# Local attention on TensorE: values and softmax sums as one burst per block pair, with long sums between value rounds 3 and 4 and in PSUM banks of their own

## The chip, the cores and the metric

The kernel runs on one core of a Trainium2 chip. The metric is the device time of one execution in microseconds (us). Every profiled run was classed as fast, with a granted TensorE clock of 0.998 or more, so all runs can be compared. TensorE appears in the profile as PE (matmuls) and PEld (weight loads), VectorE as DVE, ScalarE as ACT.

## The reference, cut to what matters

The output is `g * a + (1 - g) * b` with x of 2048 tokens by 1024 features, 32 heads of 32. `a` is a linear-attention block, `b` a local attention. Only `b` is touched:

```python
# b: local, dilated attention: each position sees 8 positions, 2 apart
logits = einsum("bhsd,bhswd->bhsw", q, kg) * scale          # W = 8, dil = 2
logits = where(mask, logits, -1e9)
attn = softmax(logits, axis=-1)
o = einsum("bhsw,bhswd->bhsd", attn, vg)
return o.transpose(...).reshape(B, S, D) @ wo
```

The kernel splits the tokens into even and odd ones, so that a window is 8 neighbours, and works in pairs of blocks of 57 queries against 64 keys. There are 18 such pairs.

## The kernel before

All matmuls are recorded as operations with a cost in a small planner, which orders them by list scheduling. Attention bursts are strewn between the groups of 8 projection matmuls (128x512), which are the bulk of the work. A pair has a burst of logits (S, 64 matmuls) and, three planner slots later, a burst of values and sums (PV). A third kind of small burst (kv, 32 matmuls) belongs to the linear attention.

In PV the array is used in tiles of 64 rows by 32 columns (how the array is split is called its mode; the projections use it whole): `h` (which block of the pair) picks the rows, `j` the columns, so 8 tiles work side by side. A head's values take 57 columns on one tile. The sums are matmuls with a stationary block of ones.

```python
SO = banks[4:8]                       # four PSUM banks, used by S and then by PV
...                                   # S: logits, Exp on ACT, mask on DVE -> E
def values():
    for g in range(2):                # two halves of the heads
        def each(e, g=g):
            for c in range(4):
                for j in range(4):
                    for h in range(2):
                        hd = 16 * g + 4 * c + j
                        e.matmul(SO[2*g + h].ap(c*nq, (c+1)*nq)[32*j:32*j+32, :],
                                 vt[64*h:64*h+64, hd*32:hd*32+32],
                                 E[64*h:64*h+64, (8*j+4*g+c)*nq:(8*j+4*g+c+1)*nq],
                                 start=True, stop=True, tile_position=(64*h, 32*j))
            for j in range(4):
                for h in range(2):    # sums of 4 heads: 228 columns, same bank as the values
                    last = e.matmul(SO[2*g + h].ap(4*nq, 8*nq)[32*j:32*j+32, :],
                                    ones[64*h:64*h+64, :],
                                    E[64*h:64*h+64, (8*j+4*g)*nq:(8*j+4*g+4)*nq], ...)
            return last               # the semaphore is incremented with this one
        P.op("pe", each, 0.36, mode="c", ...)
        P.op("act", ... Ln of the sums ...)      # both banks of the half
        P.op("act", ... Exp(-Ln) ...)
        P.op("dve", ... values * that -> qT ...)
after(PVLAG, values)
```

(Cuts are marked with dots.)

## Time and profile before

| | before |
|---|---|
| time, median of 3 runs | 504.89 us (504.59 to 505.67) |
| profiled span | 502.5 us |
| PE busy | 488.5 us, 97% of the span |
| the chain that ended last | 95% PE |

From the page of the kernel before, part 1 (busy time by engine) and the first line of part 4 (the chain that ended last):

```profile
PE 488.5 (97%) x5190; PEld 232.6 (46%) x5257; DVE 264.6 (53%) x456; ACT 192.9 (38%) x335; POOL 6.6 (1%) x30
PE 95%; issue 2%; DMA 1%; ACT 1%; SPq 0%; DVE 0%
```

TensorE is the only engine that counts. ACT and DVE are idle half the time, and their idle time costs nothing.

The timeline of PE around the first PV burst (start in us, length in us, engine, line, operation, count):

```profile
133.06 0.81 PE L1324 MATMUL ps_all<-xT,w 128*128 128x512 bf16 x3
133.80 0.31 PE L1447 MATMUL ps_all<-E,v 64*32 64x57 bf16 x32
134.02 0.33 PE L1452 MATMUL ps_all<-E,ones 64*32 64x228 bf16 x8
134.12 0.47 PE L1447 MATMUL ps_all<-E,v 64*32 64x57 bf16 x32
134.41 0.32 PE L1452 MATMUL ps_all<-E,ones 64*32 64x228 bf16 x8
134.89 3.40 PE L1324 MATMUL ps_all<-xT,w 128*128 128x512 bf16 x15 [0.16 <-issue]
138.22 0.70 PE L1427 MATMUL ps_all<-qT,kT 32*64 32x57 bf16 x64
```

L1324 are projections, L1447 values, L1452 sums, L1427 the S burst. The 0.16 us of "issue" is no wait: 16 weight loads stand against 15 matmuls there, so the record of the first matmul is missing. Merged lines hide what matters inside a burst, so the single records are needed. These are the start times of the 80 matmuls of this burst, in ns from its first weight load, eight to a line, worked out from the trace:

```
before     0: 2 5 9 12 15 19 21 25            values g=0
           8: 40 44 48 51 54 57 61 64
          16: 69 73 77 80 83 85 90 94
          24: 99 102 106 109 111 114 119 125
          32: 225 234 243 251 259 268 275 284   sums g=0
          40: 323 340 348 356 359 364 370 373   values g=1
          48: 379 380 387 389 394 404 412 420
          56: 426 434 443 451 459 468 476 484
          64: 507 528 536 544 553 561 569 604
          72: 612 620 629 637 645 653 662 670   sums g=1
projections' first weight load: 864
```

The first 32 load/matmul pairs (64 instructions) start within 0.13 us. Then there is a hole of 0.10 us, and from there pairs come at about 8.3 ns each, with further small holes. The whole burst is 0.670 us from first to last start, then 0.194 us pass until the first projection load. I call the first number the burst and the second the exit. All 18 bursts of this kernel agree within 4 ns.

### The profile page before, as it was taken

How to read it: one execution, taken by the hardware profiler on the slowest of the kernel's cores; microseconds unless marked ns; L12 is line 12 of the kernel's file. 1: busy time of each engine (PE TensorE's matmuls, PEld its weight loads, DVE VectorE, ACT ScalarE, POOL GpSimd, SP SyncE). 2: the span in 40 equal slices, each digit the busy share in tenths (PEclk: the TensorE clock that was granted, in tenths of full speed). 3: DMA queues.
4: the chain of work that ended last, by engine and by line, in shares of the span. 5: the costliest groups of instructions: out<-in, count | busy, mean ns of one | idle time of the engine just before them, and what ended most of it. 6: DMA issues, size and time to landing. Idle time of an engine off the chain costs nothing.

```text
span 502.5 us, 11582 instructions
## 1 busy us (share of the span) xinstructions
PE 488.5 (97%) x5190; PEld 232.6 (46%) x5257; DVE 264.6 (53%) x456; ACT 192.9 (38%) x335; POOL 6.6 (1%) x30
## 2 busy tenths in 40 slices
PE   8999999999999999999999999999999999999996
PEld 2444444444454444544544545444444444444443
DVE  3112235556667676454555464678776563234443
ACT  1111111111354454655554555479864543100000
POOL 5000000000000000000000000000000000000000
PEclk9999999999999999999999999999999999999999
DMA  8999990000024060100010100500000000011222
GB/s 222 207 204 314 353 270 1 1 0 1 12 86 139 22 198 27 34 23 23 23 39 21 33 1 3 170 0 1 0 2 0 2 0 1 1 43 64 83 78 73
DMA packets 47410, 34.92 MB, mean 69 GB/s; under 512 B 22261, under 2 KB 43125, under 8 KB 47354
## 3 DMA queue, kind: packets, MB, share of 16 engines
q1 hardware_dynamic: 46810, 33.59, 23.6%
q8 instruction: 43, 0.70, 0.6%
q10 hardware_dynamic: 544, 0.52, 0.4%
q14 instruction: 13, 0.11, 0.1%
HBM read 21.51 MB, written 8.40 MB: 60 GB/s over the span
## 4 chain that ended last, share of the span: by engine, by line
PE 95%; issue 2%; DMA 1%; ACT 1%; SPq 0%; DVE 0%
PE ps_all L1324 76%; PE ps_all L1677 11%; PE ps_all L1427 2%; PE ps_all L1447 2%; PE ps_all L1602 1%; PE ps_all L1452 1%; PE ps_all L1523 1%; DMA xT<-in_A_x_dram 1%; PE ps_all L1580 1%; ACT ra L1604 0%; PE ps_all L1392 0%; SPq L1294 0%; SPq L1299 0%; ACT e L1333 0%; ACT ra L1605 0%
## 5 line engine op out<-in xcount | busy, mean ns | idle before, releaser
L1324 PE MATMUL ps_all<-w,xT 128*128 128x512 bf16 x922 | 207.8, 379 | 5.6 <-issue 4.0
L1324 PE MATMUL ps_all<-xT,w 128*128 128x512 bf16 x747 | 169.2, 379 | 2.5 <-issue 1.9
L1324 PEld LDWEIGHTS ps_all<-w,xT 128*128 128x128 bf16 x960 | 91.3, 98 | 110.3 <-issue 1.7
L1324 PEld LDWEIGHTS ps_all<-xT,w 128*128 128x128 bf16 x768 | 73.9, 98 | 88.8 <-ACT ra L1604 0.6
L1677 PE MATMUL ps_all<-w,qT 128*128 128x512 bf16 (+1 forms) x259 | 55.2, 373 | 0.3
L1677 PEld LDWEIGHTS ps_all<-w,qT 128*128 128x128 bf16 x264 | 25.8, 98 | 29.7
L1335 DVE TENSOR_SCALAR e<-e 128x512 bf16<-128x512 bf16 x64 | 18.4, 291 | 38.9 <-ACT e L1331 25.3
L1355 DVE CAST vst<-ps_all 128x512 bf16<-128x512 f32 x15 | 10.4, 691 | 42.7 <-PE ps_all L1324 42.7
L1433 ACT ACTIVATE E<-ps_all 128x1824 bf16<-128x1824 f32 (+1 forms) x18 | 30.4, 1687 | 3.1 <-PE ps_all L1427 2.0
L1331 ACT ACTIVATE e<-ps_all 128x512 bf16<-128x512 f32 x32 | 19.1, 597 | 31.6 <-PE ps_all L1324 30.8
L1333 ACT ACTIVATE e<-ps_all 128x512 bf16<-128x512 f32 x32 | 19.2, 601 | 29.3 <-PE ps_all L1324 27.8
L1681 DVE SCALAR_TENSOR_TENSOR o<-ps_all,gm,xT 128x512 bf16<-128x512 f32 (+1 forms) x25 | 18.2, 729 | 23.0 <-PE ps_all L1677 22.8
L1280 DVE TENSOR_TENSOR mx<-mx,kT 128x1024 bf16<-128x1024 bf16 x32 | 20.7, 688 | 16.9 <-ACT kT L1356 16.8
L1280 DVE TENSOR_TENSOR mx<-mx,qT 128x1024 bf16<-128x1024 bf16 x32 | 20.7, 688 | 16.7 <-ACT qT L1359 16.6
L1356 ACT ACTIVATE vst<-ps_all 128x512 bf16<-128x512 f32 x17 | 10.1, 597 | 47.8 <-PE ps_all L1324 47.8
L1436 DVE TENSOR_TENSOR E<-E,msk 128x1824 bf16<-128x1824 bf16 (+1 forms) x18 | 19.8, 1100 | 14.5 <-ACT E L1433 14.5
L1462 DVE TENSOR_TENSOR qT<-ps_all,L 128x456 bf16<-128x456 f32 (+1 forms) x36 | 21.1, 624 | 7.7 <-ACT L L1461 7.7
L1359 ACT ACTIVATE qT<-ps_all 128x512 bf16<-128x512 f32 x15 | 9.0, 597 | 37.0 <-PE ps_all L1324 37.0
L1337 DVE SCALAR_TENSOR_TENSOR pk<-ps_all,e 128x512 bf16<-128x512 f32 x32 | 22.0, 688 | 0.8
L1604 ACT ACTIVATE ra<-ps_all,eps 128x512 f32<-128x512 f32 x32 | 21.5, 688 | 2.2 <-PE ps_all L1602 2.0
L1356 ACT ACTIVATE az<-ps_all 128x512 bf16<-128x512 f32 x19 | 11.4, 600 | 27.6 <-PE ps_all L1324 27.6
L1356 ACT ACTIVATE kT<-ps_all 128x512 bf16<-128x512 f32 x14 | 8.4, 597 | 35.5 <-PE ps_all L1324 35.5
(77 smaller groups left out, 336.5 us busy)
## 6 DMA issues: line engine op xcount, KB each, us to landing
w<-in_A_wqkv_dram SPq DMA_DIRECT2D x6, 1024.0 KB, 8.2
v<-vB_hbm SPq DMA_DIRECT2D x36, 128.0 KB, 2.6
vB_hbm<-vst SPq DMA_DIRECT2D x32, 128.0 KB, 4.9
w<-in_B_wqkv_dram SPq DMA_DIRECT2D x4, 1024.0 KB, 8.3
out_dram<-o SPq DMA_DIRECT2D x15, 256.0 KB, 2.0
w<-in_A_wo_dram SPq DMA_DIRECT2D x2, 1024.0 KB, 5.6
w<-in_B_wo_dram SPq DMA_DIRECT2D x2, 1024.0 KB, 6.5
w<-in_B_wqkv_dram SPq DMA_DIRECT2D x6, 256.0 KB, 4.1
```

The source lines that it names most:

```text
L1280: P.op("dve", lambda e, m=m, op=op: e.tensor_tensor(m[:, 0:n], m[:, 0:n], src, op), 0.08 + n / 1920.0, reads=[m.all(), reg], writes=[m.all()],
L1324: last = e.matmul(bank.ap(), lhs(dc), rhs(dc), start=(dc == 0), stop=(dc == 7))
L1331: P.op("act", lambda e: e.activation(e_[:, :], bank.ap(), ACT.Exp), act(512), reads=[bank.iv], writes=[e_.all()])
L1333: P.op("act", lambda e: e.activation(e_[:, :], bank.ap(), ACT.Exp, accum_out=qe[:, col:col + 1]), act(512) + 0.1, reads=[bank.iv], writes= ...
L1335: P.op("dve", lambda e: e.tensor_scalar(e_[:, :], e_[:, :], 1.0, 1e-6, op0=ALU.min, op1=ALU.add), 0.25, reads=[e_.all()], writes=[e_.all()])
L1337: P.op("dve", lambda e: e.scalar_tensor_tensor(out=dst, in0=bank.ap(), scalar=0.0, in1=e_[:, :], op0=ALU.max, op1=ALU.add), dps(512), read ...
L1356: fa = lambda e: e.activation(dst, src(), ACT.Copy)
L1433: P.op("act", lambda e: e.activation(E[:, 0:32 * nq].rearrange("p (j q) -> p j q", j=4), ps[:, 4:8, 0:8 * nq], ACT.Exp), act(32 * nq), rea ...
L1436: P.op("dve", lambda e: e.tensor_tensor(ev(), ev(), m[:, :, :].rearrange("p r q -> p (r q)")[:, None, :].to_broadcast([128, 16, 2 * nq]), ...
L1462: P.op("dve", lambda e, L=L, pb=pb, g=g: e.tensor_tensor(qT[:, 4 * g:4 * g + 4, t0 + qs:t0 + qs + 2 * nq].rearrange("p c (h q) -> p h c q" ...
L1604: P.op("act", lambda e: e.activation(R[:, :], db.ap(), ACT.Ln, bias=eps[:, :]), act(512), reads=[db.iv, eps.all()], writes=[R.all()])
L1677: last = e.matmul(bank.ap(0, f1 - f0), qT[:, dc, t * 128:(t + 1) * 128], ws[3][:, dc, f0:f1], start=(dc == 0), stop=(dc == 7))
```

## The change

Its intent is to spend less PE time on a pair: the two halves become one burst and one operation, sums of 4 heads (228 columns, 16 matmuls) become sums of 8 heads (456 columns, 8 matmuls), and these stand between value rounds 3 and 4 (a round is 8 values, one on each tile). 456 columns of values and 456 of sums do not fit into one bank, which the kernel lays out as 512 columns, so values go to banks 0 and 1 of the four and sums to banks 2 and 3. Ln, Exp and multiply go by block `h` instead of by half of the heads, in the same number and size. The planner's cost of the burst changes from 2 x 0.36 to 0.61 us, so the order of instructions is planned anew.

```diff
-    Lr = Ring([SB([128, 2, 4 * 57], F32, "L%d" % i) for i in range(2)])
+    Lr = Ring([SB([128, 8 * 57], F32, "L%d" % i) for i in range(2)])
+    SUMS_AT = 3
 ...
-                for g in range(2):
-                    def each(e, g=g):
-                        for c in range(4): ...            # values, as shown above
-                        for j in range(4): ...            # sums, as shown above
-                        return last
-                    P.op("pe", each, 0.36, mode="c", ..., writes=bi, name="PV")
+                def each(e):
+                    def part(c):
+                        for j in range(4):
+                            for h in range(2):
+                                hd = 4 * c + j
+                                last = e.matmul(SO[h].ap(c * nq, (c + 1) * nq)[32 * j:32 * j + 32, :], vt[64 * h:64 * h + 64, hd * 32:hd * 32 + 32],
+                                                E[64 * h:64 * h + 64, (8 * j + c) * nq:(8 * j + c + 1) * nq], start=True, stop=True, tile_position=(64 * h, 32 * j))
+                        return last
+                    for c in range(SUMS_AT):
+                        part(c)
+                    for j in range(4):
+                        for h in range(2):
+                            e.matmul(SO[2 + h].ap(0, 8 * nq)[32 * j:32 * j + 32, :], ones[64 * h:64 * h + 64, :], E[64 * h:64 * h + 64, 8 * j * nq:8 * (j + 1) * nq],
+                                     start=True, stop=True, tile_position=(64 * h, 32 * j))
+                    for c in range(SUMS_AT, 8):
+                        last = part(c)
+                    return last
+                P.op("pe", each, 0.61, mode="c", ..., writes=[s.iv for s in SO], name="PV")
+                for h in range(2):
 ...                                                         # Ln, Exp, multiply by h instead of g
```

More of the change, by code (lines that the diff above doesn't have):

```diff
@@ L1439, in values @@
             def values():
-                for g in range(2):
-                    def each(e, g=g):
-                        for c in range(4):
-                            for j in range(4):
-                                for h in range(2):
-                                    hd = 16 * g + 4 * c + j
-                                    e.matmul(SO[2 * g + h].ap(c * nq, (c + 1) * nq)[32 * j:32 * j + 32, :], vt[64 * h:64 * h + 64, hd * 32:hd * 32 + 32],
-                                             E[64 * h:64 * h + 64, (8 * j + 4 * g + c) * nq:(8 * j + 4 * g + c + 1) * nq],
-                                             start=True, stop=True, tile_position=(64 * h, 32 * j))
+                def each(e):
+                    def part(c):
@@ L1450, in each @@
                         for j in range(4):
                             for h in range(2):
-                                last = e.matmul(SO[2 * g + h].ap(4 * nq, 8 * nq)[32 * j:32 * j + 32, :], ones[64 * h:64 * h + 64, :],
-                                                E[64 * h:64 * h + 64, (8 * j + 4 * g) * nq:(8 * j + 4 * g + 4) * nq],
-                                                start=True, stop=True, tile_position=(64 * h, 32 * j))
-                        return last
-                    bi = [SO[2 * g].iv, SO[2 * g + 1].iv]
@@ L1457, in values @@
-                    P.op("pe", each, 0.36, mode="c", reads=[vt.all(), ones.all(), E.all()], writes=bi, name="PV")
-                    L, _ = Lr.next()
-                    pb = lambda o, g=g: ps[:, 4 + 2 * g:6 + 2 * g, 4 * o * nq:4 * (o + 1) * nq]
-                    P.op("act", lambda e, L=L, pb=pb: e.activation(L[:, :, 0:4 * nq], pb(1), ACT.Ln), act(8 * nq), reads=bi, writes=[L.all()])
-                    P.op("act", lambda e, L=L: e.activation(L[:, :, 0:4 * nq], L[:, :, 0:4 * nq], ACT.Exp, scale=-1.0), act(8 * nq), reads=[L.all()], writes=[L.all()])
@@ L1462, in values @@
-                    P.op("dve", lambda e, L=L, pb=pb, g=g: e.tensor_tensor(
-                        qT[:, 4 * g:4 * g + 4, t0 + qs:t0 + qs + 2 * nq].rearrange("p c (h q) -> p h c q", h=2),
-                        pb(0).rearrange("p h (c q) -> p h c q", c=4), L[:, :, 0:4 * nq].rearrange("p h (c q) -> p h c q", c=4), ALU.mult), dps(8 * nq),
-                        reads=bi + [L.all()], writes=[qT.part((4 * g, 4 * g + 4), (t0 + qs, t0 + qs + 2 * nq))])
+                                hd = 4 * c + j
@@ new lines, in each @@
+                    for c in range(SUMS_AT, 8):
+                        last = part(c)
+                    return last
+                P.op("pe", each, 0.61, mode="c", reads=[vt.all(), ones.all(), E.all()], writes=[s.iv for s in SO], name="PV")
+                for h in range(2):
+                    L, _ = Lr.next()
+                    n = 8 * nq
+                    P.op("act", lambda e, L=L, h=h: e.activation(L[:, 0:n], SO[2 + h].ap(0, n), ACT.Ln), act(n), reads=[SO[2 + h].iv], writes=[L.all()])
+                    P.op("act", lambda e, L=L: e.activation(L[:, 0:n], L[:, 0:n], ACT.Exp, scale=-1.0), act(n), reads=[L.all()], writes=[L.all()])
+                    q0 = t0 + qs + h * nq
+                    P.op("dve", lambda e, L=L, h=h, q0=q0: e.tensor_tensor(
+                        qT[:, :, q0:q0 + nq], SO[h].ap(0, n).rearrange("p (c q) -> p c q", c=8), L[:, 0:n].rearrange("p (c q) -> p c q", c=8), ALU.mult), dps(n),
+                        reads=[SO[h].iv, L.all()], writes=[qT.part((0, 8), (q0, q0 + nq))])
```

## The prediction

> **What bounds the kernel.** TensorE. The page gives PE 97% of a 502.5 us span, the chain that ended last is 95% PE, the granted clock is full. The list of waits shows no PE wait on ACT or DVE in the attention stage (128 to 315 us). So a change pays only by what it takes out of the PE stream.
>
> **What one pair costs now.** In the timeline a pair's values and sums are one unbroken stretch: 32 value matmuls, 8 sums of 228 columns, 32 values, 8 sums, with 80 weight loads. From the single PE records (first pair, 133.79 us; all 18 alike):
> - entry: 0.09 us;
> - the first 32 load/matmul pairs start within 0.12 us;
> - a hole of 0.10 us before the next matmul (first sum);
> - then about 8.3 ns per pair, with a 39 ns hole where values wait for the first sums, and late holes of 23, 20 and 34 ns; last matmul at 0.67 us;
> - 0.19 us until the projections' first weight load: about 0.095 us of the last sum's columns, 0.10 us of drain.
> About 0.97 us of PE, 17.5 us for 18 pairs (3.5% of the span).
>
> The 32 fast pairs are 64 instructions. The Trainium skill, "TensorE: Matmul & The Clock Gate", table at its head, gives the engine's queue as 64 deep; the trace agrees (the hole comes after matmul 32 in PV and in S). So instruction issue bounds the burst, not columns.
>
> **What the change does.** Columns stay the same. 8 weight loads and 8 matmuls fall away: 8 x 8.3 ns = 0.066 us. Three rounds of values and the 8 long sums are exactly 64 instructions, so they issue from the full queue, and the refill hole (0.10 us) lies under the sums' stream. A sum of 228 columns held its tile 98 ns (first sum to next value), so one of 456 should hold it about 195 ns (estimate), from about 0.10 to 0.29 us. The other 40 value pairs become available at 8.3 ns each from 0.225 us, so the last starts at about 0.55 us, or 0.60 if the late holes stay. The burst now ends in a 57-column matmul, as S does, whose exit is 0.135 us, not 0.19: 0.06 us less. New cost 0.79 to 0.84 us a pair; saving 0.12 to 0.18 us, times 18: 2.2 to 3.3 us, all on the critical path.
>
> **What it could cost.** Ln starts only when the whole burst is done, so the last multiply should end 0.2 us later. Today it ends 1.17 us or more before the next S burst, so S should not wait. ACT and DVE work keeps its size (36 Ln of 0.55, 36 Exp of 0.59, 36 multiplies of 0.62 us). The order is planned anew with other costs, so a kv burst now next to PV may move (each separate one costs some 0.2 us more).
>
> **Prediction.** 502.3 us, 80% range 501.0 to 503.7. Faster by over 2%: 0.01; within 2%: 0.98; slower by over 2%: 0.01.
>
> **What the profile should show.** 72 matmuls per burst, the hole after the 32nd hidden in the sums' stream, 0.55 to 0.60 us from first to last start, first projection load 0.135 us later; S bursts unchanged at 0.50 us; no PE wait on ACT or DVE.
>
> **What would make it wrong.** Sums that block weight loads for all tiles, so that the refill does not run under them; a new order that adds mode changes or waits for banks; a late Ln chain delaying S.

## The result

The changed kernel took 501.80 us (median of 4 runs, 501.19 to 502.48) against 504.74 us for the kernel before (504.45 to 505.67, 4 runs). The ratio is 0.9942, with a 95% interval of 0.9928 to 0.9956. Here and below a ratio is the mean time of one kernel's fast runs over that of the other's of the same rounds, so it is not quite the ratio of the medians quoted. The gain is real and well inside 2%.

From the page of the changed kernel, the lines that answer to those above:

```profile
PE 493.2 (99%) x5113; PEld 231.4 (46%) x5113; DVE 267.6 (54%) x460; ACT 191.4 (38%) x331; POOL 6.6 (1%) x30
PE 96%; SPq 2%; DMA 1%; ACT 1%; issue 0%; DVE 0%
```

PE's busy time went up although the kernel got faster. That is no contradiction: the kernel before lacks about 70 matmul records, and this trace lacks none (as many matmuls as weight loads). Busy PE time is the wrong number here; the length of each stretch is the right one. The timeline of PE around the first PV burst after (L1325 projections, L1447 values, L1454 sums):

```profile
133.03 0.81 PE L1325 MATMUL ps_all<-xT,w 128*128 128x512 bf16 x3
133.76 0.28 PE L1447 MATMUL ps_all<-E,v 64*32 64x57 bf16 x24
133.86 0.38 PE L1454 MATMUL ps_all<-E,ones 64*32 64x456 bf16 x8
134.06 0.51 PE L1447 MATMUL ps_all<-E,v 64*32 64x57 bf16 x40
134.49 5.35 PE L1325 MATMUL ps_all<-xT,w 128*128 128x512 bf16 x24
```

And its single records, in ns as before:

```
after      0: 1 5 8 11 15 18 21 25            values, rounds 0 to 2
           8: 41 44 46 50 54 57 60 63
          16: 70 73 76 79 83 86 89 92
          24: 99 102 105 108 111 115 120 124    sums, 456 columns
          32: 291 294 296 300 303 306 311 316   values, rounds 3 to 7
          40: 317 321 323 326 330 334 342 351
          48: 359 367 376 384 392 401 409 417
          56: 476 484 492 501 509 517 526 534
          64: 542 551 559 567 576 584 592 601
projections' first weight load: 724
```

The burst fell from 0.670 to 0.601 us and the exit from 0.194 to 0.123 us: 0.140 us a pair.

That accounts for the whole gain. I measured from the 257th projection weight load (after the v projections) to the 1280th (after the last PV burst; one separate kv burst comes later): 256.35 us before, 253.77 us after, 2.58 us less. (The ratio above stands for 2.9 us, with 2.2 to 3.6 us for its interval; the two profiled spans differ by 2.4 us.) Sixteen pairs give 0.140 us each and the two pairs with a kv burst directly ahead give 0.104 us each, 2.45 us together. There is also one separate stretch of bursts between projections fewer (38 against 39), because one more kv burst came to stand next to a PV burst; the lengths of the stretches put that at 0.10 us. Ahead of the measured part and behind it, the two traces agree within 0.2 us.

The risk of a late Ln did not come true. From the timelines of ACT and DVE, the Ln, Exp and multiply of the first pair before and after (L1460, L1461, L1462 became L1463, L1464, L1466):

```profile
134.38 0.99 ACT L1460 ACTIVATE L<-ps_all 128x456 f32<-128x456 f32 x2 [1.61 <-PE ps_all L1452]
135.26 1.06 ACT L1461 ACTIVATE L<-L 128x456 f32<-128x456 f32 x2
135.88 1.17 DVE L1462 TENSOR_TENSOR qT<-ps_all,L 128x456 bf16<-128x456 f32 x2
```

```profile
134.64 0.99 ACT L1463 ACTIVATE L<-ps_all 128x456 f32<-128x456 f32 x2 [1.90 <-PE ps_all L1447]
135.52 1.06 ACT L1464 ACTIVATE L<-L 128x456 f32<-128x456 f32 x2
137.04 1.16 DVE L1466 TENSOR_TENSOR qT<-ps_all,L 128x456 bf16<-128x456 f32 x2
```

Ln starts 0.26 us later and the multiply over a microsecond later in this pair, yet the next S burst begins 1.58 us after the multiply's end here, and never less than 1.05 us after it in any pair. The waits of PE after the change name no engine in the attention stage:

```profile
PE ps_all L1364 <- DVE warm L1273: 1.3, 1, 1.3
PE ps_all L1325 <- DMA xT<-in_A_x_dram: 0.9, 2, 0.7
```

Both of these stand at the start of the kernel.

### The profile page after: what moved, and what is told of

Its sections match the earlier page's. It is cut to its first block, busy times and chain, and to the rows that moved or that the text cites. A ratio compares the mean times of both kernels' runs of the same rounds, so it can differ in the third digit from the quotient of the medians.

```text
span 500.1 us, 11359 instructions
## 1 busy us (share of the span) xinstructions
PE 493.2 (99%) x5113; PEld 231.4 (46%) x5113; DVE 267.6 (54%) x460; ACT 191.4 (38%) x331; POOL 6.6 (1%) x30
## 4 chain that ended last, share of the span: by engine, by line
PE 96%; SPq 2%; DMA 1%; ACT 1%; issue 0%; DVE 0%
PE ps_all L1325 76%; PE ps_all L1680 11%; PE ps_all L1428 2%; PE ps_all L1447 2%; PE ps_all L1605 1%; SPq L1295 1%; PE ps_all L1526 1%; DMA w<-in_B_wqkv_dram 1%; PE ps_all L1454 1%; PE ps_all L1583 1%; SPq L1300 1%; ACT ra L1607 0%; PE ps_all L1393 0%; ACT e L1334 0%; ACT ra L1608 0%
## 5 line engine op out<-in xcount | busy, mean ns | idle before, releaser
L1325 PE MATMUL ps_all<-w,xT 128*128 128x512 bf16 x960 | 214.2, 379 | 1.1 <-DMA xT<-in_A_x_dram 0.9
L1325 PE MATMUL ps_all<-xT,w 128*128 128x512 bf16 x768 | 172.1, 379 | 0.1
L1325 PEld LDWEIGHTS ps_all<-w,xT 128*128 128x128 bf16 x960 | 91.1, 98 | 109.9 <-DMA w<-in_B_wqkv_dram 1.4
L1325 PEld LDWEIGHTS ps_all<-xT,w 128*128 128x128 bf16 x768 | 74.1, 98 | 88.8 <-ACT ra L1607 0.6
L1466 DVE TENSOR_TENSOR qT<-ps_all,L 128x456 bf16<-128x456 f32 (+1 forms) x36 | 21.0, 627 | 6.2 <-ACT L L1464 5.0
L1463 ACT ACTIVATE L<-ps_all 128x456 f32<-128x456 f32 (+1 forms) x36 | 17.8, 547 | 12.4 <-PE ps_all L1447 12.4
L1359 DVE TENSOR_SCALAR xT<-ps_all,g 128x512 bf16<-128x512 f32 x15 | 11.2, 750 | 19.9 <-PE ps_all L1325 19.9
```

Source lines behind the costliest of these rows:

```text
L1325: last = e.matmul(bank.ap(), lhs(dc), rhs(dc), start=(dc == 0), stop=(dc == 7))
L1466: P.op("dve", lambda e, L=L, h=h, q0=q0: e.tensor_tensor(qT[:, :, q0:q0 + nq], SO[h].ap(0, n).rearrange("p (c q) -> p c q", c=8), L[:, 0:n ...
```

## The experiments

The total was forecast well, but the reason had parts that total time cannot tell apart: fewer pairs, the place of the sums, their banks, one operation instead of two, the last matmul's length. Also unexplained was the late hole of 59 ns ahead of matmul 56 above. Twelve kernels were run, each with a profile and five timed rounds. Times of one kernel differ by 0.5 to 2.6 us from run to run, so for the finer points I read the burst and the exit from the trace, where the bursts of one kernel agree within some 10 ns (apart from the two or three with a kv burst directly ahead, which are left out of these numbers, and one burst of tail that was 28 ns longer). The tables give the first pair's burst and exit, for tail the typical one.

### Where the sums stand: rounds 4, 0 and 8

```diff
-    SUMS_AT = 3
+    SUMS_AT = 4        # run pos4;  0 in run pos0,  8 in run pos8
```

In pos8 the last sum also carries the increment. Instruction order and all other engines' programs are the same as in the changed kernel.

> The changed kernel with the sums between value rounds 4 and 5 instead of 3 and 4, nothing else. Theory LINE (the burst's length is set by the rate at which load/matmul pairs reach the array after the 32 queued ones: last start = 0.225 us + 8.3 ns for each pair beyond 32 + about 0.05 us of late holes; the sums' place does not matter as long as their stream ends before that): burst 0.60 us from first to last start as in the changed kernel, within 0.02 us, and 501.8 us. Rival COVER (what the prediction said: the change gains because 24 values and 8 sums are exactly the 64 queued instructions and the refill hole of 0.10 us lies under the sums' stream): here the hole falls bare after 32 values, the burst is 0.70 us and the time 1.8 us longer, 503.6 us.

> The changed kernel with the sums ahead of all values. LINE: the sums hold all tiles for 0.195 us at the start, the 24 queued value pairs follow at under 4 ns each, up to about 0.30 us, the refill goes on meanwhile, and the last start is at 0.60 us again: 501.8 us. COVER (and a refill that begins only when the queue has run empty): the hole of 0.10 us stands bare after the 24th value, at about 0.30 us, and 40 pairs at 8.3 ns follow: last start at 0.73 us, 2.3 us longer in all, 504.1 us.

> The changed kernel with the sums after all values, so that the burst ends in 456 columns. LINE: first to last start still 0.60 us (72 pairs), but the exit grows by the columns that the last sum streams[...], so about 0.29 us from the last matmul to the first projection load; 18 x 0.17 = 3.0 us longer, 504.8 us. COVER: the bare hole of 0.10 us as well, 1.8 us on top, 506.6 us.

| sums ahead of round | burst, us | exit, us | time, us (median) | ratio to before |
|---|---|---|---|---|
| 3 (the change) | 0.601 | 0.123 | 501.80 | 0.9942 |
| 4 (pos4) | 0.674 | 0.123 | 503.19 | 0.9974 (0.9954 to 0.9994) |
| 0 (pos0) | 0.717 | 0.123 | 503.74 | 0.9984 (0.9966 to 1.0003) |
| 8 (pos8) | 0.551 | 0.289 | 504.03 | 0.9990 (0.9971 to 1.0008) |

(The three were run beside the kernel before at 504.22 us, the change beside it at 504.74 us.)

LINE fell: the place matters, by up to 0.12 us a pair. COVER came near in pos4 and pos0, but fell in pos8 (506.6 us forecast, 504.03 measured; LINE said 504.8). LINE's rate, without its late holes, is exact where the sums come last: in pos8 the burst has no late hole at all, 72 pairs end at 0.551 us, which is 0.226 us plus 39 x 8.3 ns. And there the exit grows by 0.166 us for 399 columns more (the 0.17 us expected is scaled from the 98 ns for which a sum of 228 columns held its tile in the kernel before). The exits after 57, 228 and 456 columns (0.123, 0.194 and 0.289 us) lie on a line: 0.416 ns a column and a rest of 0.10 us. That is how the prediction split its 0.19 us; that the rest is a drain is not seen in a trace. So the base rate was right, and something that the sums do adds to it. My next theory, HOLD, was that a tile held by a streaming sum stops the supply of instructions for good.

### Count of matmuls and banks: two228, oldbanks, oneop, tail

two228 keeps place and banks of the change, but cuts each sum in two:

```diff
-                    for j in range(4):
-                        for h in range(2):
-                            e.matmul(SO[2 + h].ap(0, 8 * nq)..., ones..., E[..., 8 * j * nq:8 * (j + 1) * nq], ...)
+                    for f in range(2):
+                        for j in range(4):
+                            for h in range(2):
+                                e.matmul(SO[2 + h].ap(4 * f * nq, 4 * (f + 1) * nq)..., ones..., E[..., (8 * j + 4 * f) * nq:(8 * j + 4 * f + 4) * nq], ...)
```

> The changed kernel, same place and own banks, but each sum of 8 heads as two matmuls of 228 columns (80 pairs instead of 72, the same columns). LINE: 8 pairs more at 8.3 ns, burst 0.66 to 0.67 us, exit unchanged at 0.124 us; 18 x 0.066 = 1.2 us longer, 503.0 us. Rival BANKS (the gain comes of the sums having banks of their own, or of one burst instead of two, and the count of matmuls is of no weight): burst 0.60 us, 501.8 us.

oldbanks has the same order of matmuls as two228, but the banks, Ln, Exp and multiply of the kernel before: `SO[2 * g + h]` for values and sums of half g.

> The kernel before with its values and sums as one burst in the order of the changed kernel (three rounds of values, 16 sums of 228 columns, five rounds of values), but each pair of banks still shared by the values and sums of a group, and Ln, Exp and multiply by group as before. HOLD: the same as the run with two sums of 228 columns in banks of their own, burst 0.64 us, exit 0.124 us, 502.8 us. Rival BANKS (own banks for the sums are needed for the gain): burst 0.67 us and an exit of 0.19 us as before, 504.5 us.

oneop is the kernel before with its two operations joined:

```diff
-                for g in range(2):
-                    def each(e, g=g):
-                        ...
-                    P.op("pe", each, 0.36, ..., writes=bi, name="PV")
+                def each(e):
+                    for g in range(2):
+                        ...
+                P.op("pe", each, 0.61, ..., writes=[s.iv for s in SO], name="PV")
+                for g in range(2):
```

> The kernel before with its two halves of a burst joined to one operation (one semaphore increment at the end, Ln only after all), in the same order of matmuls, layout and banks. In the run with two sums of 228 columns, 80 pairs took 0.642 us; the kernel before takes 0.670 us for 80 pairs with a hole of 34 ns between matmuls 70 and 71 that that run lacks. If joining is what removes it: 0.643 us, exit 0.19 us, 18 x 0.027 = 0.5 us less than before. If the join is of no weight: 0.670 us and the time before.

tail is the kernel before with its last two rounds turned:

```diff
-                        for c in range(4): values(c)
+                        for c in range(4 - g): values(c)
                         ... sums ...
+                        if g == 1: last = values(3)
```

> The kernel before with only its last two rounds turned: the last round of values after the last 8 sums, so that the burst ends in 57 columns. HOLD: the exit shrinks from 0.194 to 0.124 us, but the last values wait for the sums' tiles (98 ns of stream against 66 ns of issue), 0.03 us longer to the last start: a net gain of 0.04 us, 0.7 us in all. Rival: the exit is no part of the gain, 0.19 us as before, time as before or 0.5 us longer.

| run | burst, us | exit, us | sum | time, us (before beside it) | ratio |
|---|---|---|---|---|---|
| before | 0.670 | 0.194 | 0.864 | 504.74 | 1 |
| oneop | 0.643 | 0.194 | 0.837 | 504.20 (504.51) | 0.9992 (0.9980 to 1.0004) |
| oldbanks | 0.643 | 0.123 | 0.766 | 502.75 (504.51) | 0.9966 (0.9953 to 0.9979) |
| two228 | 0.643 | 0.123 | 0.766 | 502.78 (504.22) | 0.9970 (0.9950 to 0.9989) |
| after | 0.601 | 0.123 | 0.724 | 501.80 (504.74) | 0.9942 (0.9928 to 0.9956) |
| tail | 0.701 | 0.113 | 0.814 | 503.37 (504.51) | 0.9981 (0.9966 to 0.9996) |

Read from top to "after", this is a ladder from one kernel to the other, one part at a step:

- Joining the operations is worth 0.027 us. It removes one increment in mid-burst. By time alone oneop cannot be told from the kernel before (its interval includes 1); the step is seen in the trace.
- Taking the last sums away from the end is worth 0.071 us, all of it in the exit.
- Banks of their own are worth nothing by themselves. BANKS fell: two228 and oldbanks agree. They are only the price of sums that are 456 columns long.
- Eight long sums in place of 16 short ones are worth 0.042 us, and not the 8 x 8.3 = 0.066 us of the pairs saved; half, below, shows why.

From oneop down to the change the planned order also has the kv burst that moved next to PV (0.10 us in all); before and tail do not. The columns "burst" and "exit" are free of that, the times are not.

The timelines of oneop and of oldbanks show the step in the exit (L1324 projections, L1447 or L1446 values, L1452 or L1454 sums):

```profile
133.74 0.31 PE L1447 MATMUL ps_all<-E,v 64*32 64x57 bf16 x32
133.96 0.32 PE L1452 MATMUL ps_all<-E,ones 64*32 64x228 bf16 x8
134.06 0.45 PE L1447 MATMUL ps_all<-E,v 64*32 64x57 bf16 x32
134.32 0.32 PE L1452 MATMUL ps_all<-E,ones 64*32 64x228 bf16 x8
134.57 1.25 PE L1324 MATMUL ps_all<-xT,w 128*128 128x512 bf16 x5
```

```profile
134.11 0.28 PE L1446 MATMUL ps_all<-E,v 64*32 64x57 bf16 x24
134.21 0.45 PE L1454 MATMUL ps_all<-E,ones 64*32 64x228 bf16 x16
134.43 0.52 PE L1446 MATMUL ps_all<-E,v 64*32 64x57 bf16 x40
134.88 1.04 PE L1324 MATMUL ps_all<-xT,w 128*128 128x512 bf16 x4
```

From the first value to the first projection there are 0.83 us in the first and 0.77 us in the second.

The run tail shows the exit by itself, on the kernel before: it falls from 0.194 to 0.113 us. The burst grows by 0.031 us, because the last values now wait for the tiles that the last sums hold, so 0.050 us a pair are left, about as HOLD expected (0.04).

### Is it the held tile? stag

stag places the sums so that no value ever comes to a tile whose sum still streams:

```diff
-                    for c in range(SUMS_AT): part(c)
-                    ... all 8 sums ...
-                    for c in range(SUMS_AT, 8): last = part(c)
+                    A, B = (0, 1), (2, 3)                 # tiles by j
+                    for c in range(3): vals(c, A + B)
+                    sums(A)
+                    for c in range(3, 6): vals(c, B)
+                    sums(B)
+                    for c in range(3, 8): vals(c, A)
+                    for c in range(6, 8): last = vals(c, B)
```

> The changed kernel with its eight sums in two groups of four: rounds 0 to 2 of all tiles, sums of tiles j=0,1, rounds 3 to 5 of tiles j=2,3, sums of j=2,3, rounds 3 to 7 of j=0,1, rounds 6 and 7 of j=2,3. The same 72 pairs, columns and banks; no value comes to a tile whose sum is still streaming. Theory HOLD (formed after the first four runs: with no held tile, 72 pairs take 0.55 us, as in the run with sums last; each time the next matmul's tile is held by a sum, the hold is lost for good; between rounds 3 and 4 that is 0.05 us): burst 0.55 us, exit 0.124 us, 0.05 us a pair less than the changed kernel, 18 x 0.05 = 0.9 us, 500.9 us, ahead of both kernels. Rival BUBBLE (the late hole of 0.05 us in the changed kernel comes of something else, as of instruction fetch at that place): burst 0.60 us, 501.8 us.

The burst was 0.605 us and the exit 0.121 us; the time was 502.23 us (before 504.51 us, ratio 0.9955, 0.9942 to 0.9968). HOLD fell. Nothing is held any more, matmul 32 starts at 225 ns in place of 291, and yet the hole ahead of matmul 56 stands exactly where it was:

```
stag      32: 225 234 242 250 259 270 279 286
          40: 295 304 313 320 325 334 342 350
          48: 361 370 379 389 395 404 412 420
          56: 477 485 494 502 510 522 530 539
```

So the hole belongs to pair 56, and in the change and in stag pair 24 is the first long sum. Its record lasts 0.350 us, from 99 to 449 ns, and pair 56 starts at 476 ns. With that, all earlier holes fell into place: a pair starts about 27 ns after the end of the matmul 32 pairs ahead of it. I call this WINDOW.

### Tests of WINDOW: pos2, pos5, half, stag2

pos2 and pos5 are the change with `SUMS_AT` 2 and 5. half cuts the sums to 228 columns without changing their count:

```diff
-   e.matmul(SO[2 + h].ap(0, 8 * nq)..., ones..., E[..., 8 * j * nq:8 * (j + 1) * nq], ...)
+   e.matmul(SO[2 + h].ap(0, 4 * nq)..., ones..., E[..., 8 * j * nq:(8 * j + 4) * nq], ...)
-   e.activation(L[:, 0:n], SO[2 + h].ap(0, n), ACT.Ln)
+   e.activation(L[:, 0:n] as (2, n/2), SO[2 + h].ap(0, n // 2) read twice, ACT.Ln)
```

stag2 places two groups of sums by the new rule:

```diff
                     for c in range(3): vals(c, A + B)
-                    sums(A)
-                    for c in range(3, 6): vals(c, B)
-                    sums(B)
-                    for c in range(3, 8): vals(c, A)
-                    for c in range(6, 8): last = vals(c, B)
+                    vals(3, A)
+                    sums(B)
+                    for c in range(4, 8): vals(c, A)
+                    sums(A)
+                    for c in range(3, 8): last = vals(c, B)
```

> The changed kernel with the sums between value rounds 2 and 3. Theory WINDOW (formed after eight runs; it takes the place of HOLD): besides tiles held by a sum and 8.3 ns a pair, a load/matmul pair can start only some 27 ns after the end of the matmul 32 pairs ahead of it, as the trace has that end. This gives the hole after the 32nd pair (first value 0.198 us long) and the late hole (a sum of 456 columns 0.350 us long, 24 pairs later in the changed kernel as its 32nd follower is pair 56). Here: sums start at 0.066 us as pairs 16 to 23, round 3 is held until about 0.26 us, pairs 32 to 47 catch up, and a hole stands between pairs 47 and 48, which starts at 0.066 + 0.350 + 0.027 = 0.443 us; the last start is at 0.635 us. Rival EMPTY (the supply starts anew 0.10 us after the queue has run out, and lost time stays lost): pair 32 at 0.39 us, last start at 0.72 us.

> The changed kernel with the sums between value rounds 5 and 6, as pairs 40 to 47. WINDOW: no pair has one of the sums 32 pairs ahead of it, so there is no late hole; the next values are held by their tiles until about 0.487 us and the 24 left follow at about 5 ns each: last start at about 0.61 us. HOLD (held time is lost in full): 0.55 + 0.13 = 0.68 us.

> The changed kernel with every sum cut to the first 228 of its 456 columns, and Ln reading those twice (a wrong result on purpose: heads 16 to 31 are divided by the sums of heads 0 to 15). The 72 pairs, their places and the rest of the work stay. WINDOW: a sum of 228 columns ends 0.266 us after its start, so pair 56 may start at 0.099 + 0.266 + 0.027 = 0.39 us, before its turn at 0.425 us: no late hole, burst 0.55 us, 0.9 us less in all than the changed kernel. Rival BUBBLE (the late hole comes of instruction fetch at that place in the burst): 0.60 us as in the changed kernel.

> The changed kernel with its sums in two groups placed by WINDOW: rounds 0 to 2 of all tiles, round 3 of tiles j=0,1, sums of tiles j=2,3 (pairs 28 to 31), rounds 4 to 7 of j=0,1, sums of j=0,1 (pairs 48 to 51), rounds 3 to 7 of j=2,3. WINDOW: the late hole moves to pairs 59/60, where pair 60 starts at 0.112 + 0.350 + 0.027 = 0.489 us in place of 0.458, so the last start is at 0.58 us; 0.02 us a pair better than the changed kernel, 0.3 us in all, too little to tell by time. BUBBLE: hole of 0.05 us between pairs 55 and 56, last start 0.60 us.

| run | burst expected by WINDOW | burst measured | exit, us | time, us (before 504.36) | ratio |
|---|---|---|---|---|---|
| pos2 | 0.635, hole ahead of 48 | 0.640, hole ahead of 48 | 0.124 | 502.79 | 0.9969 (0.9956 to 0.9983) |
| pos5 | 0.61, no late hole | 0.609, none | 0.116 | 502.06 | 0.9955 (0.9941 to 0.9968) |
| half | 0.55, no late hole | 0.551, none | 0.125 | 500.88 | 0.9930 (0.9916 to 0.9943) |
| stag2 | 0.58, hole ahead of 60 | 0.582, hole ahead of 60 | 0.122 | 502.05 | 0.9955 (0.9941 to 0.9969) |

All four bursts came within 5 ns of what was written before they ran, and EMPTY (0.72 us for pos2), HOLD (0.68 us for pos5) and BUBBLE (0.60 us for half and stag2) are each off by about 0.02 to 0.08 us. The timeline of half, to be set against that of the change above, shows the same counts in the same places in less time:

```profile
133.70 0.28 PE L1447 MATMUL ps_all<-E,v 64*32 64x57 bf16 x24
133.80 0.28 PE L1454 MATMUL ps_all<-E,ones 64*32 64x228 bf16 x8
133.93 0.52 PE L1447 MATMUL ps_all<-E,v 64*32 64x57 bf16 x40
134.61 1.24 PE L1325 MATMUL ps_all<-xT,w 128*128 128x512 bf16 x5 [0.16 <-issue]
```

(The 0.16 us is again a missing record.) The wrong sums of half passed the comparison with the reference. I take it that the logits are so small that all heads' sums are nearly equal; the kernel is wrong all the same and is no candidate.

The rule, read from single records of eight kernels (ns from the first load of the burst; "end" is the end of the record, which the profile models):

```
kernel  pair   end of the matmul 32 ahead   start   difference
before    32   199 (value)                   225       26
before    64   479 (sum, 228 columns)        507       28
before    71   550 (sum, with increment)     604       54
oneop     71   550 (sum, no increment)       577       27
after     56   449 (sum, 456 columns)        476       27
pos0      32   365 (sum, 456 columns)        392       27
pos2      48   421 (sum, 456 columns)        448       27
pos4      64   576 (sum, 456 columns)        604       28
two228    64   479 (sum, 228 columns)        506       27
stag2     60   461 (sum, 456 columns)        489       28
```

The S burst obeys it too: its first matmul ends at 211 ns and pair 32 starts at 238 ns. And it holds as a floor everywhere: of the 18,864 pairs in the PV and S bursts of all 14 traces that have another one 32 ahead, none starts sooner than 26 ns after the recorded end of that one. Counted 31 ahead there is no such floor: some start over 70 ns before the end. Since each matmul here has its own weight load, the runs cannot tell 32 matmuls from 64 instructions.

stag, stag2 and pos5 show the rule's reach past the burst. In 11 of 18 pairs a kv burst follows PV directly. There the stretch from the last projection weight load ahead of PV to the first one behind kv is 1.557 us in the change and 1.59 us in these three, although PV alone is not longer. No kv pair starts right behind the end of a sum, but an estimate from the single records, made after the runs, fits: the pair 32 behind the last sum is supplied 27 ns after that sum's end, each later one 8.3 ns after the one before, and PV's increment adds 27 ns ahead of the last kv pair. In pos5 the last sum (pair 47) ends at 712 ns and the last kv pair is 24 after pair 79, so it should start at 712 + 27 + 24 x 8.3 + 27 = 965 ns; in stag and stag2 the same sum gives 964 and 966 ns. Measured were 965, 963 and 965 ns, and 929 ns in the change. No run tested this. It would explain why stag2, with a burst 0.02 us shorter, is not faster in all. None of the placements tried beats the change in time; the best correct ones are equal to it within their intervals.

## Why the prediction was right

- **TensorE bounds the kernel, and only PE time counts.** Right. The stretch with the attention bursts shortened by 2.58 us, and the bursts account for 2.55 us of it.
- **0.97 us a pair before, 0.79 to 0.84 us after.** Right. Entry, burst with exit, and the start of the first projection matmul are 0.09 + 0.724 + 0.01 = 0.83 us after, where the same reading gave 0.09 + 0.864 + 0.01 = 0.97 us before.
- **8 pairs fewer save 0.066 us.** The term is right, but 0.024 us of it are given back, since the first long sum's record of 0.350 us (0.255 us in two228 and half) holds back the pair that comes 32 later. That late hole costs 0.050 us in the change (0.601 us against 0.551 in half), and late holes cost 0.027 us in two228 (0.643 us against 0.226 + 47 x 8.3 ns = 0.616). two228 against the change measures 0.042 us net.
- **The hole lies under the sums' stream.** Right as far as it goes. The sums hold their tiles until 291 ns, of which the hole until 225 ns is free; at round 4 (pos4) it stands bare, the sums end later and hold back pair 64, and the burst is 0.073 us longer.
- **The queue's refill runs on its own from 0.225 us.** This was the weak step. The prediction took the hole for a refill after 64 queued instructions, in agreement with the depth of 64 that the Trainium skill gives ("TensorE: Matmul & The Clock Gate", table at its head). The number fits, but the refill does not run on its own: the runs show that a pair starts no sooner than about 27 ns after the end of the matmul 32 pairs ahead, so a long sum stops it 32 pairs later. The "late holes" that the prediction left open ("0.60 if the late holes stay") are this. That the burst came out at 0.601 us is in part luck: the old late holes did not stay. They cost about 0.05 us beyond the 8.3 ns pace, half of it from the increment that is gone; one new hole of 0.050 us, from a sum twice as long, took their place.
- **The exit falls to 0.135 us.** Right; it fell to 0.123 us, the largest single part of the gain, 0.071 us a pair.
- **Not in the prediction: 0.027 us from one increment fewer.** The Trainium skill's "TensorE: Matmul & The Clock Gate", "The cost: per-tile semaphore tail", puts each increment at about 26 ns, in a formula for the time after a group of tiles. The trace agrees in size: pair 71 starts 54 ns in place of 27 ns after the end of the matmul with the increment, and oneop has no such hole. In oneop the boundary between two operations went together with the increment, so the two were not tested apart.
- **The new order.** One kv burst more stands next to a PV burst, worth 0.10 us and not the 0.2 us estimated.
- **Ln's chain does not delay S.** Right; 1.05 us or more are left. That the multiply would end only 0.2 us later was wrong for the first pair, where it starts 1.16 us later behind a cast on DVE, but there was room for it.

By the ladder, the 0.140 us of a pair are 0.071 us exit, 0.042 us longer sums in fewer matmuls and 0.027 us one operation. Each is the difference of two runs that are neighbours in the ladder. That the 27 ns rule is due to the queue giving up a place at a matmul's end is an inference from the records and from the four forecasts that came true; the ends are modelled by the profile, and no run looked into the queue itself. What sets 8.3 ns a pair once the queue is used up is also open.

## What to carry to other kernels

For a burst of many small matmuls on tiles, count load/matmul pairs and not columns: in this kernel 32 were quick, the others cost 8.3 ns each, and none started before the one 32 ahead of it had ended, so a long matmul is paid for 32 pairs later unless the burst is over by then. End a burst with short matmuls: here the exit ahead of the next mode was 0.123 us after 57 columns and 0.289 us after 456. When a change moves several such things at once, walk from one kernel to the other one part at a time and read burst and exit from single records: 0.03 us a pair is invisible in one time of 500 us and plain in 18 equal bursts.

## What the Trainium skill lacked or had wrong

- "TensorE: Matmul & The Clock Gate", table at its head, gives a queue of 64 with a partial reorder window. It does not say when a place comes free. Here a pair starts 26 to 28 ns after the end of the matmul 32 pairs ahead, in nine of the ten cases listed, and 54 ns after one that carries an increment; none of 18,864 pairs in all traces starts sooner than 26 ns after.
- No page has the rate at which load/matmul pairs follow once those 64 are used up: 8.3 ns a pair here. "TensorEngine Tiling (Array Packing)", "Instruction Overhead", speaks of about 60 cycles for each matmul and does not say whether that holds across tiles; in these bursts on 8 tiles pairs started 3 to 4 ns apart while queued and 8.3 ns apart afterwards.
- "TensorEngine Tiling (Array Packing)", "Key Properties", says that a change of tiling mode drains the array but gives no time. Here the next mode's first weight load came 0.123 us after the start of a last matmul of 57 columns (0.11 to 0.125 us over all PV bursts that end so), 0.194 us after one of 228 and 0.289 us after one of 456.
- "TensorE: Matmul & The Clock Gate", "The cost: per-tile semaphore tail", describes the cost of increments as a tail. Here a single increment in mid-burst (before against oneop) cost 27 ns, 32 pairs later, and only there.
